# Hash projections of the first batch in float32 from the raw loads, one operation for both lower halves, leaner constants and a new list of places

## The chip, the core and the metric

The kernel runs on one core of a Trainium2 chip. The metric is the device time of one execution in microseconds (us); the shorter, the better. Beside the runs there is one profiled execution, from which all rows below are taken. The engines are TensorE (PE, with its weight loads as PEld), VectorE (DVE), ScalarE (ACT), GpSimd (POOL) and SyncE (SP), which issues most DMAs.

## What is computed

Bucketed attention (4 batches, 8 heads, 768 positions, head width 64), and behind it a feed-forward layer on the 3072 tokens. Cut from the reference:

```python
q_bits = (np.einsum('bhsd,dk->bhsk', q, proj) > 0)      # proj is 64 x 6
k_bits = (np.einsum('bhsd,dk->bhsk', k, proj) > 0)
q_bucket, k_bucket = sum(bits * 2**arange(6))
mask = q_bucket[..., :, None] == k_bucket[..., None, :]
scores = where(mask, 1/8 * q @ k.T, -1e9)
attn = softmax(scores); out = attn @ v                  # then, on (3072 x 512):
h = x @ w_in; g = gelu(h); y = g @ w_out                # w_in 512 x 2048
```

## The kernel before

**Precision.** Everything is float32 at the boundary. A matmul operand is either kept as float32, or held as two parts, an upper and a lower half: for q and k in the type fp32r (tiles `Aq`, `Ak` for the upper, `Bq`, `Bk` for the lower halves), for v, the attention weights and the feed-forward in f16.

**Steps and the list of places.** The program doesn't emit its instructions where it describes them. It describes 3,604 steps (`add`), each with the steps it needs, the engines that could do it, and the ring of buffers it takes a slot of. `Plan.order` then reads the string `ORDER`: three characters for each step, in the order in which the steps were added. The first two are its place (base 64), the third its engine and slot (`ENGINES[way // 8]`, `way % 8`). The steps are emitted in the order of their places, so each engine and each DMA queue gets its instructions in that order and works them off in that order.

**Stages.** The first batch (8 heads) runs through `head_early`, the other three through `head`. Beside the first batch the weights are decoded, scaled and split (`weight_pair`), almost wholly on DVE. Then the feed-forward of a batch is laid between the attention steps of the following batches, and the last batch's feed-forward ends the program.

**One head of the first batch** (`head_early`, L656 on). `raw` is loaded (L664): 128 rows, q above and k below, 768 columns, in one of two single buffers (`raw` for odd heads, `rawe` for even ones). `hi` writes the upper halves of q (times -1/8) and k to `aq`. Three moves (`m1`, `m2`, `m3`) copy halves of `aq` to where the matmuls want them; `lq` and `lk` (L685, L394) write the two lower halves, 64 rows each. The projection (L722 to L724) is three fp32r matmuls that add up in one bank, in two pieces of 256 and 512 columns, with `first_lo`, `first_hi` as weights; a sign on ACT (L727) follows each piece, with the bias `off`; two mask steps `r1`, `r2` write the bits under q and k. The scores (L846) of the head need `m3`, `r1` and `r2`, the projection needs `m1`, `m2`, `lq` and `lk`. `raw` is free when `lq` and `lk` have read it.

**One unit of 128 queries** (`unit`): scores on PE (L846), the least on DVE (L849), exp on ACT (L854); in the first batch then six transposes on PE (L904) with copies out by ACT or DVE (L925), and the product with v in float32 (L984).

**Constants** (L302 to L331): `proj` is sent to 2 x 64 rows by one DMA from ACT's queue (`praw`), `offset` to 2 x 32 rows of one 4-byte word by a second one (`off`). POOL makes `first_hi` and `first_lo` from `praw` with four operations. Two steps (`hash_parts`, `flip_parts`, L419 to L442) make constants for the heads of the later batches from `praw` and `off`.

Of the kernel before, what the change touches and what calls it, by code (L numbers as in the profile page):

```python
# [18 lines left out]
P = 128  # L19
# [4 lines left out]
RAWE = 1  # L24
WHOLE = ((0, 1, 2, 3), (), (), ())
# [9 lines left out]
    "HyYASIAFgAZBAdgAvAAzgBNABSgBuAB2IB7QCABCFICSICYIClIBVgADgAIIAJQALQANQAKIAMIAPoAUBAXQAQAAVQAYQAaIAeAAnIAtQAxoBEABGQA+DBMQ"  # L35
    "AkBArIAwRA2AA4QA9ABAQAyAA5IBDRBHpBLCBZQBTDBcIA3BBBIBJQBjDBnQBQABWQBIABPIBeRBiqBsCBvQBtDByQBUBBgIBpQB1CB+QB4DCCQAEgAOIAbI"
    "AhQAcQATIAWIAmoAqCA7QAsDA1QBOQBCYBlABqIB0RB9rCHDCbQCLACUIBxBB6ICGQCaAChQCWCCeICgQCjICzIC1BC5QAAoCnACsACwADFIDoQDwYCBACKI"
    "CTRC3oDBBDJQDCCDLQCPBCmICtQC6DDDQC4CC8QC2QC7IDZQDfADmRABpDSCDYADcADuIEAQEMYCcACqIDAQDErDMDDdQDQBDbQDIADPIDWQDnBDrQDhDDkQ"
    "DsQD0ID9ID-DECQACqDxBD1AEQAEYIEgYEiYE5hARgAlQApYAoQBRYAuIBFIBYoBbABhQBfCBmQCNQBrYC-BDjIDzQD5pEBAENQEGDEJQDiADpID7REaCEnQ"
    "EWAEbQD8BELIETQEZoEkBEsQEoAEqQEKAEUIEhRExBFAQEtCFBQEeBEmIEuQEzqE6AFEQFCDFHQEpAEvIE4RFGCF3QFFBFSQAggA6YBdYCMYCEgBKIB3YCVo"  # L40
    "CXBCdQCiDCoQDOYCxQE8AFDIFKQFNrFjDFmQFTAFaQE1BE+IFMRFbBFhQFgAFkQFdIFpIFyIF9CF-RFqDFtAFxAGRIGnQHEYFOAFXIFoQF1pGMCGbIF2BF8Q"
    "FWBFeIFsRGECGGQGUDGgQFwIF5IGIYGLAGPIGrBGzAG5AG-IHhIHrYF6AGJIGQQGXrGcAGiQGfBGlQGFBGTIGaRGmDGuIGoCHHQG2QG7IHAYHcDHfRHNCHoA"
    "HuAH2IICIIGYFigBagCRYCkQCvgDTgCZICfYDUoDtAD4QDqDDvQERYEEQGhBGwIG3RG+oHGBHMQHQAHVQGYAGeIGyQHFAHKQHCDHRQG9AHDIHOQHSpHXBHbQ"
    "HnAHwIHIBHPIHWRHmBHqQHiDH0QHdBHpIHvQH1qH6BIHQH9DIAQHUAHjIHsRH4AH8QIDDISQCJgDeQD6gEVYFUgEFIDlYEfoEyDE7QFLDFVQF0QFvQHxAH5I"
    "IBQIIrIOAIUIIMBIfQH+BIEIILRIWCIbQIYDIeIIRQIdIIoIIvCI7QIwBI2AI5AJBIKQQKnYIKAIPIIVQI-oJCDJHQJGBJLIIQBIXIIhRJNDJSQJQBJgQItY"
    "I1II4QI9CJDRJrAJwAJzAJ7IKcQKiYIcAIsIJKQJTrJeAJhQJYDJdQImBI3IJXRJoDJ1QJkBJqQJ6IKSIKUQKqBKvRKIAKLAKhAK1IMLQMMIKohCrgEwYE3g"
    "E9gFZgFQIE-YF4oF+BGDQGOBGWQHBQGpQJUAJnIJuQJ5pKFCKXQJ-BKNQJfBJtIJyRJ+CKAQKBAKEQKCAKGIKKQKOoKpCKsQKRDKWQJ4BKDIKHRKeDKjQKYB"
    "KgQKVAKdIKmRKtqK3BK7QK6DK9QKPBKlIKxQLDALWQLACLEQEOgGNYG0gGxgHkQGkIGVYHLoHYAHgQIFCINQITYIZYKyAK4IK-RLFrLLBLPQLGDLMQK8BLCI"
    "LKQLNCLSQLRDLUQLVQLjILmQLtDLyQLYBLfALlAL0IMGIMJYLHALZILhQLqpLsALuQLvCLzQLTBLeILoRL2DL8QL6CL-IL1QL4IMAQMIDMNQMKBMQAMaAMfI"
    "MtQNPILpALwIL3QL9rMFCMTQL+BMDQLxBL5IMERMdDMhQMRDMXQMYQMiIMsQM+CNLRNIDNOANSANaIP8QSMIAHhAGgAfIAjIA0IBoAAiiA8gBXIBkIBwIB8A"  # L50
    "CDICIICOBCQICpICyIC9IDNQDaIDGYDVIA-hB5iCuIC0IC+IEDCDHhB-gDgID2ID+IEIAESIEXQEdDEjIE0IFIIFPIFYYFrIFfYGAIEHgDXiErIE2IFJIFnA"
    "EPhFRiFuIFzIF7IGCAGHIGKYGSAGZIGdIGjIGsIGvYG1IG6QHZIGBhFcgG8IHJIHTIIaAG4iHegH-IIJIIiIIrAIyII8QJICJOIJbIJiIJmIJpYKrIJvYJ9I"
    "HahIpgJEIJRIJcIKuDJPiJlgKJIKMIKTIKwAK0IK2QK5ALBILIILOILXILcQLkILbYLrIJ2hKfiK+ILJILQIL7AKkgLaiMCIMPIMWIMlAMnIMrQMuCMxIM0I"
    "M6IM8INCQNfINMQNTILghMciMzIM2INBINnDMegNGhNWINdINkINwAN0IN2QN5DN7IOBIOGIOHIOJYOuIORIOoIOkgNJiO8IPBIPEIPwAO5hPKgPYIPcIPnI"
# [136 lines left out]
def tile_bucket_attention_moe(  # L191
# [465 lines left out]
    def head_early(b, h, i, key, clear, cl):  # L657
# [78 lines left out]
        def mask_q():  # L736
            affine(r1.engine, aq[D : D + 2 * NBIT], buf(space)[: 2 * NBIT], 0.5, 0.5)
# [629 lines left out]
```

## Time and profile before

| | us |
|---|---|
| median of 3 runs | 855.67 |
| lowest and highest | 855.56, 857.36 |
| the profiled execution: its own time | 856.2 |
| its span in the trace | 854.4 |

Over the span PE is busy 833.5 us (98%), DVE 681.1 (80%), ACT 641.4 (75%), POOL 69.4 (8%). A busy share of PE is not PE at its peak: the ends of matmuls are modelled, and starts tell the pace better. Times in the rows are us from the start of the span unless they are marked ns.

### The profile page before, as it was taken

To read this page: it belongs to the slowest core of one execution; us is meant where nothing else is said; L and a number is where in the kernel's file an instruction comes from. 1 tells how busy PE (TensorE), PEld (TensorE's weight loads), DVE (VectorE), ACT (ScalarE), POOL (GpSimd) and SP (SyncE) were. 2 spreads that over 40 slices of the span, in tenths; PEclk is the share of its full clock that TensorE was granted. 3 is DMA by queue.
4 is the path that set the end of the run, shared out by engine and by line. 5 is a ranking of instruction groups with operands and counts; after the bars stand their busy time and mean duration, and the time that the engine had idled before them with its cause. 6 is when DMAs were issued, how large, how long until landed. Compare 5 with 4: busy or idle time off the path is not lost.

```text
span 854.4 us, 16603 instructions
## 1 busy us (share of the span) xinstructions
PE 833.5 (98%) x6428; PEld 609.5 (71%) x6428; DVE 681.1 (80%) x1392; ACT 641.4 (75%) x1091; POOL 69.4 (8%) x81
## 2 busy tenths in 40 slices
PE   5899999999999999999999999999999999999998
PEld 3676777857777776777676777677777777676664
DVE  7999999998999999998999989899898771212112
ACT  6898998889898998888988868988878754323232
POOL 3453320102000000000000000000000000000000
PEclk9999999999999999999999999999999999999999
DMA  6775465691996898697979696668869454001000
GB/s 207 224 200 147 148 188 165 130 188 38 187 166 139 164 193 215 118 194 134 185 160 194 165 169 129 150 134 156 182 126 178 94 108 78 1 1 50 2 25 25
DMA packets 270018, 116.56 MB, mean 136 GB/s; under 512 B 228596, under 2 KB 253172, under 8 KB 269940
## 3 DMA queue, kind: packets, MB, share of 16 engines
q1 hardware_dynamic: 269744, 115.50, 61.7%
q8 instruction: 50, 0.82, 0.4%
q14 instruction: 28, 0.23, 0.1%
q10 hardware_dynamic: 196, 0.00, 0.0%
HBM read 41.95 MB, written 6.29 MB: 56 GB/s over the span
## 4 chain that ended last, share of the span: by engine, by line
PE 86%; DVE 6%; DMA 4%; ACT 2%; issue 1%; ACTq 0%; SPq 0%; DVEq 0%
PE hp L1275 28%; PE hp L1196 27%; PE s L846 14%; PE hp L993 8%; PE hp L984 3%; PE hp L904 3%; DVE s L849 2%; PE hp L798 1%; PE hp L799 1%; DMA off<-offset 1%; ACT p L854 1%; DMA wbits<-w_out 1%; DMA vraw<-v 1%; PE hp L505 1%; DMA pt<-hl 1%
## 5 line engine op out<-in xcount | busy, mean ns | idle before, releaser
L1275 PE MATMUL hp<-Wout,g 128*128 128x512 f16 x1152 | 278.5, 380 | 0.0
L1196 PE MATMUL hp<-x,Win 128*128 128x256 f16 x2304 | 272.5, 273 | 0.0
L1196 PEld LDWEIGHTS <-Win 128*128 128x128 f16 x2304 | 219.9, 98 | 46.6 <-issue 11.2
L849 DVE TENSOR_SCALAR_CACHE_REDUCE s<-s 128x768 f32<-128x768 f32 x192 | 182.9, 958 | 14.1 <-PE s L846 12.0
L1275 PEld LDWEIGHTS <-g 128*128 128x128 f16 x1152 | 103.2, 98 | 115.5 <-issue 18.8
L854 ACT ACTIVATE p<-s,rows 128x768 f32<-128x768 f32 x144 | 129.5, 900 | 27.5 <-DVE s L849 10.0
L846 PE MATMUL s<-Ak,Aq 128*128 128x384 f32 x360 | 145.2, 403 | 4.8 <-ACT p L854 3.5
L1206 ACT ACTIVATE h<-hp,ffs 128x512 f32<-128x512 f32 x96 | 65.1, 683 | 98.7 <-PE hp L1196 96.7
L846 PE MATMUL s<-Bk,Bq 128*128 128x384 f32 x360 | 122.0, 339 | 0.0
L1253 DVE SCALAR_TENSOR_TENSOR g<-h,ffs,g 128x512 f16<-128x512 f32 x96 | 70.5, 744 | 28.2 <-ACT g L370 27.1
L846 PEld LDWEIGHTS s<-Ak,Aq 128*128 128x128 f32 x360 | 68.6, 190 | 22.7 <-ACT p L854 7.7
L373 DVE TENSOR_SCALAR g<-h,ffs 128x512 f16<-128x512 f32 x39 | 18.5, 481 | 82.8 <-ACT h L1231 76.5
L993 PE MATMUL hp<-pt,vhl 128*64 128x256 f16 x1296 | 76.1, 274 | 0.0
L993 PEld LDWEIGHTS <-vhl 128*64 128x64 f16 x1296 | 68.7, 110 | 8.4 <-issue 7.8
L846 PEld LDWEIGHTS s<-Bk,Bq 128*128 128x128 f32 x360 | 68.8, 191 | 1.8
L854 ACT ACTIVATE wbits<-s,rows 128x768 f32<-128x768 f32 x48 | 43.1, 898 | 14.1 <-DVE s L849 5.4
L869 DVE SCALAR_TENSOR_TENSOR wbits<-p,rows,wbits 128x768 f16<-128x768 f32 x47 | 47.4, 1011 | 3.6 <-ACT wbits L370 3.3
L869 DVE SCALAR_TENSOR_TENSOR hl<-p,rows,hl 128x768 f16<-128x768 f32 x49 | 49.4, 1009 | 0.3
L1231 ACT ACTIVATE h<-h 128x2048 f32<-128x2048 f32 (+1 forms) x25 | 46.1, 1843 | 0.4
L904 PE MATMUL hp<-ident,p 128*128 128x128 f32 x288 | 43.0, 277 | 0.4 <-ACT pt L370 0.3
L370 ACT ACTIVATE pt<-hp 128x384 f32<-128x384 f32 x86 | 39.1, 490 | 4.5 <-PE hp L904 4.0
L370 ACT ACTIVATE g<-h,ffs 128x512 f16<-128x512 f32 x56 | 39.1, 713 | 1.2 <-PE hp L1275 1.0
(196 smaller groups left out, 1041.4 us busy)
## 6 DMA issues: line engine op xcount, KB each, us to landing
raw<-qk SPq DMA_DIRECT2D x28, 384.0 KB, 4.0
vraw<-v SPq DMA_DIRECT2D x28, 384.0 KB, 4.0
wbits<-w_in SPq DMA_DIRECT2D x16, 512.0 KB, 4.7
wbits<-w_out SPq DMA_DIRECT2D x16, 512.0 KB, 5.0
out<-o SPq DMA_DIRECT2D x11, 512.0 KB, 3.6
Ak<-Aq SPq DMA_DIRECT2D x16, 192.0 KB, 3.3
Bq<-Aq SPq DMA_DIRECT2D x13, 192.0 KB, 3.6
Bk<-Aq SPq DMA_DIRECT2D x12, 192.0 KB, 4.2
```

The lines of the kernel that those rows point to most:

```text
L370: nc.scalar.activation(out=out, in_=in_, func=func, scale=scale, bias=bias)
L846: nc.tensor.matmul(to, x, y, start=k == 0, stop=k == 1)
L849: nc.vector.tensor_scalar(out=both(sp), in0=both(sp), scalar1=BIG / 2, scalar2=None, op0=ALU.min, op1=ALU.min, accum_out=nb,)
L854: nc.scalar.activation(out=buf(ex).rearrange("p (b k) -> p b k", b=2), in_=both(sp), func=AF.Exp, scale=-1.0, bias=nb, accum_out=sums[:, t ...
L869: nc.vector.scalar_tensor_tensor(out=buf(hi)[:, 1], in0=buf(ex), scalar=r, in1=buf(hi)[:, 0], op0=ALU.mult, op1=ALU.subtract,)
L904: nc.tensor.transpose(buf(step[0])[:, (k - k0) * P : (k - k0 + 1) * P], buf(ex)[:, words(k)], ident32,)
L993: nc.tensor.matmul(pv[j * D : (j + 1) * D], buf(vh)[:, tv, kt, j * D : (j + 1) * D], buf(holds[j][0])[:, tp * KT + kt, :nt], start=kt == 0 ...
L1196: nc.tensor.matmul(buf(pair[0])[:, j * ch[1] : (j + 1) * ch[1]], win_hl[:, f0 // WB1, tw, pr, f0 % WB1 : f0 % WB1 + P], x[:, tx, pr, : ch[1]],
L1206: nc.scalar.activation(out=bufs["h"][0][:, 2 * fp : 2 * fp + 2, :nt], in_=buf(pair[0])[:, : 2 * nt].rearrange("p (j k) -> p j k", j=2), fu ...
L1231: nc.scalar.activation(out=h, in_=h, func=AF.Gelu)
L1253: nc.vector.scalar_tensor_tensor(out=gt[:, 1, s2, :nt], in0=h[:, s2, :nt], scalar=sg, in1=gt[:, 0, s2, :nt], op0=ALU.mult, op1=ALU.subtract,)
L1275: nc.tensor.matmul(buf(banks[u]), gt[:, tg, f, u * P : (u + 1) * P], wout_hl[:, ft // UT, tw, ft % UT], start=fresh and f == ti == 0, stop ...
```

## The change

In the first batch all 8 heads (`EXACT = 8`, `JOINT = range(8)`) project `raw` itself with float32 weights `plain`, in one matmul for each piece, and need `raw` alone for it. Both lower halves are written by one DVE operation on 128 rows (`joint_low`) into `bq`; the lower half of k is moved from there to `bk` (`m1`, after `joint_low`), and then the upper half of q goes into the place that it left (`m4`, after `m1`). A head has 14 steps before and after, the scores now need `m1`, `m4` and `joint_low` too, and `raw` is free only when `joint_low` and both pieces of the projection have read it. `proj` is loaded to 64 rows, `offset` by two DMAs of 12 rows each behind a POOL memset; ACT writes `plain` with four operations on 64 x 6, and POOL copies it to `praw`. `flip_parts` and `hash_parts` now need the first batch's signs and projections.

```diff
+EXACT = 8
+JOINT = range(8)
 ORDER = (
...
-    nc.scalar.dma_start(out=praw[:, :NBIT], in_=proj.unsqueeze(0).to_broadcast([2, D, NBIT]))
+    nc.scalar.dma_start(out=praw[:D, :NBIT], in_=proj)
-    nc.scalar.dma_start(out=off, in_=offset.rearrange("(n p) o -> n p o", n=2)[:, :KR])
+    nc.gpsimd.memset(off, 0.0)
+    for n in range(2):
+        nc.scalar.dma_start(out=off[n * KR : n * KR + 2 * NBIT], in_=offset[n * D : n * D + 2 * NBIT])
...
-    first_hi = const.tile([P, KR + HR], F32R, tag="first_hi", name="first_hi")
-    first_lo = const.tile([P, HR], F32R, tag="first_lo", name="first_lo")
+    plain = const.tile([P, HR], F32, tag="plain", name="plain")
+    nc.vector.memset(plain, 0.0)
...
-    nc.gpsimd.tensor_scalar(
-        out=praw[:, NBIT:], in0=praw[:, :NBIT], scalar1=-1.0, scalar2=None, op0=ALU.mult
-    )
-    nc.gpsimd.tensor_copy(out=first_hi[:, KR : KR + 2 * NBIT], in_=praw)
     for rr, cc in sides:
-        nc.gpsimd.tensor_tensor(
-            out=first_lo[rr, cc], in0=praw[rr], in1=first_hi[rr, KR : KR + 2 * NBIT].bitcast(F32), op=ALU.subtract
-        )
+        for n, by in enumerate((1.0, -1.0)):
+            to = slice(cc.start + n * NBIT, cc.start + (n + 1) * NBIT)
+            nc.scalar.activation(out=plain[rr, to], in_=praw[:D, :NBIT], func=AF.Copy, scale=by)
+    for rr, cc in sides:
+        nc.gpsimd.tensor_copy(out=praw[rr], in_=plain[rr, cc])
...
+        def joint_low():
+            nc.vector.scalar_tensor_tensor(
+                out=bq, in0=buf(raw), scalar=fold, in1=aq.bitcast(F32), op0=ALU.mult, op1=ALU.subtract
+            )
...
-        m1 = add_move(S, bq[:D], aq[:D])
-        m2 = add_move(S, bk[D:], aq[D:])
-        m3 = add_move(S, ak[:D], aq[D:])
-        lq = add_low(bq[D:], top, -SCALE)
-        lk = add_low(bk[:D], end)
-        free(raw, [lq, lk])
+        if joint:
+            lows = [add("DVE", subtract_cost("DVE", S), joint_low, key, [hi], port=True)]
+            m2 = add_move(S, bk[:D], aq[D:])
+            m3 = add_move(S, ak[:D], aq[D:])
+            m1 = add_move(S, bk[D:], bq[D:], lows)
+            m4 = add_move(S, bq[D:], aq[:D], [m1])
...
-                nc.tensor.matmul(pp, first_lo, aq[:, n], start=True, stop=False)
-                nc.tensor.matmul(pp, first_hi[:, KR:], bq[:, n], start=False, stop=False)
-                nc.tensor.matmul(pp, first_hi[:, :HR], bk[:, n], start=False, stop=True)
+                nc.tensor.matmul(pp, plain, buf(raw)[:, n], start=True, stop=True)
...
+        if exact:
+            hashed.needs += products
+            flipped.needs += signs
...
+        free(raw, [*lows, *(products if exact else ())])
...
-        return [m3, r1, r2]
+        return [m3, r1, r2, *([m4] if joint else ()), *((m1, *lows) if exact else ())]
```

**What the two lists say**, read with the code of `Plan.order`. For the first head: before, DVE `hi`, `lq`, `lk`, then the second head's `hi`, `flip_parts`, its `lq`, `lk`, then `r2` and a move, then the first weight decode; after, DVE `hi`, `joint_low`, `m1`, the second head's `hi`, `m4`, `r2`, its `joint_low`, then the first weight decode. On ACT before: `m1`, `m2`, `m3`, signs, `r1`; after: the four constants, `m2`, `m3`, signs, `r1`.

Steps placed before the first evacuation of the feed-forward (place 832 before, 826 after), where the counts differ by engine:

| step | DVE before, after | ACT | POOL | SP |
|---|---|---|---|---|
| `hi` of the first batch | 2, 3 | 2, 1 | 4, 4 | |
| lower halves (`lq`, `lk`; `joint_low`) | 11, 8 | | 5, 0 | |
| moves and masks of the first batch | 2, 4 | 17, 18 | 11, 12 | 10, 14 |
| copies of transposes (L925) | 10, 7 | 86, 89 | | |
| `spread` of the divisors | 4, 2 | 6, 9 | 2, 1 | |
| upper halves of x from `rb` | 3, 1 | 7, 9 | 1, 1 | |
| moves and masks of the second batch's heads | | 2, 5 | 2, 1 | 8, 6 |
| upper halves of weights (`high_low`) | | 3, 4 | 7, 6 | |

In the whole program the numbers of steps are the same on PE. The last weight load is step 970 of the list before, its decode 984; after, the last loads are 904 and 966, the decode 992.

## Rows read from the trace of the kernel before

**Rows 1.** Windows by stage: stretch, its length, busy time and instructions of each engine.

```profile
0.00:15.00 15.00, 5.05 (x19) 3.79 (x20) 9.94 (x18) 9.23 (x12) 4.99 (x19) 1.00 0.64 215
15.00:147.50 132.50, 126.96 (x945) 97.91 (x944) 130.61 (x262) 116.66 (x256) 48.40 (x48) 1.00 0.60 176
180.00:200.00 20.00, 18.59 (x121) 11.62 (x120) 16.99 (x36) 16.50 (x24) 1.51 (x2) 1.00 0.68 174
200.00:700.00 500.00, 499.88 (x4018) 369.47 (x4016) 458.20 (x963) 423.08 (x697) 11.05 (x11) 1.00 0.77 155
700.00:854.00 154.00, 150.51 (x1059) 100.11 (x1057) 33.87 (x55) 47.94 (x59) 0.00 (x0) 1.00 0.11 28
```

**Rows 2.** Timeline of the first 14 us: start, length, engine, operation [idle before].

```profile
0.73 1.13 ACTq L302 DMA_DIRECT2D praw<-proj  x1
...
1.89 0.53 ACTq L304 DMA_DIRECT2D off<-offset  x1
...
3.74 0.20 ACT L316 ACTIVATE warm<-ones 128x1 f32<-128x1 bf16 x1
4.11 0.62 DVE L373 TENSOR_SCALAR Aq<-rawe,fold 128x768 fp32r<-128x768 f32 x1 [1.39 <-DMA rawe<-qk]
...
5.70 0.24 POOL L326 TENSOR_SCALAR praw<-praw 128x6 f32<-128x6 f32 x1 [2.07 <-DMA praw<-proj]
...
6.74 0.62 DVE L373 TENSOR_SCALAR Aq<-raw,fold 128x768 fp32r<-128x768 f32 x1
...
7.74 0.65 PE L722 MATMUL hp<-Aq,first_lo 128*44 128x512 f32 x1 [7.74 <-POOL first_lo L331]
...
8.19 0.63 PE L723 MATMUL hp<-Bq,first_hi 128*44 128x512 f32 x1
...
9.57 0.15 DVE L439 TENSOR_SCALAR flips<-off 64x1 f32<-64x1 f32 x1 [2.21 <-DMA off<-offset]
9.66 1.23 ACT L727 ACTIVATE sign<-hp,off,turned 44x512 f32<-44x512 f32 x2 [2.32 <-DMA off<-offset]
...
12.89 0.66 PE L846 MATMUL s<-Ak,Aq 128*128 128x384 f32 x1 [1.16 <-DVE Ak L373]
...
13.25 0.68 DVE L484 TENSOR_SCALAR Win<-wbits 128x1024 int32<-128x1024 int32 x1
```

**Rows 3.** Timeline of PE: the third head's projection, then a product with v.

```profile
25.31 0.32 PE L722 MATMUL hp<-x,first_lo 128*44 128x256 f32 x1
...
26.44 0.27 PE L904 MATMUL hp<-ident,p 128*128 128x128 f32 x1
...
39.05 2.81 PE L984 MATMUL hp<-pt,vhl 128*64 128x256 f32 x24
```

**Rows 4.** Groups by form, 0 to 147.5 us: busy us, mean ns | idle before.

```profile
L373 DVE TENSOR_SCALAR pt<-hp 128x384 f32<-128x384 f32 x10 | 5.5, 546 | 0.1
...
L685 DVE SCALAR_TENSOR_TENSOR Bq<-raw,Aq 64x768 fp32r<-64x768 f32 x4 | 4.7, 1174 | 0.1
...
L776 DVE SCALAR_TENSOR_TENSOR Bq<-raw,fold,Aq 128x768 fp32r<-128x768 f32 x2 | 2.0, 1010 | 0.0
...
L685 DVE SCALAR_TENSOR_TENSOR Bq<-rawe,Aq 64x768 fp32r<-64x768 f32 x2 | 1.9, 952 | 0.1
...
L373 DVE TENSOR_SCALAR Bq<-Aq 64x768 fp32r<-64x768 f32 x1 | 0.6, 552 | 0.0
...
L370 ACT ACTIVATE pt<-hp 128x384 f32<-128x384 f32 x86 | 39.1, 490 | 4.5 <-PE hp L904 4.0
...
L370 ACT ACTIVATE Ak<-Aq 64x768 fp32r<-64x768 f32 x3 | 2.5, 842 | 0.1
...
L394 POOL TENSOR_TENSOR Bk<-raw,Aq 64x768 fp32r<-64x768 f32 x3 | 5.5, 1825 | 3.6 <-ACT Aq L370 3.5
```

**Rows 5.** Timeline of DVE around 181 us.

```profile
181.45 0.76 DVE L484 TENSOR_SCALAR Wout<-wbits 128x512 int32<-128x512 int32 x2 [1.02 <-DMA wbits<-w_out]
```

**Rows 6.** DMA issues: KB each, median us to landing.

```profile
raw<-qk SPq DMA_DIRECT2D x28, 384.0 KB, 4.0
```

More of the change, by code (lines that the diff above doesn't have):

```diff
@@ L39 @@
[L39 to L42, printed above, removed]
@@ L673, in move, with add_move @@
                 affine(on, dst, src.bitcast(F32))
-        def add_move(n, dst, src):
+        def joint_low():
+            nc.vector.scalar_tensor_tensor(
+                out=bq, in0=buf(raw), scalar=fold, in1=aq.bitcast(F32), op0=ALU.mult, op1=ALU.subtract
+            )
+        def add_move(n, dst, src, needs=None):
             box = []
@@ L678, in add_move @@
             box.append(
-                add(on, 0, lambda: move(box[0].engine, dst, src), key, [hi], port=True)
+                add(on, 0, lambda: move(box[0].engine, dst, src), key, needs or [hi], port=True)
             )
@@ L706, in head_early @@
         hi = add(affine_on(f"RND{first}", S, True), 0, high, key, [raw, *clear], port=True)
-        m1 = add_move(S, bq[:D], aq[:D])
-        m2 = add_move(S, bk[D:], aq[D:])
-        m3 = add_move(S, ak[:D], aq[D:])
-        lq = add_low(bq[D:], top, -SCALE)
-        lk = add_low(bk[:D], end)
-        free(raw, [lq, lk])
-        space = add("none", 0, lambda: None, key, [m1, m2, lq, lk], takes="sign")
-        signs = []
+        exact = h < EXACT
+        joint = h in JOINT
+        if joint:
[4 more added lines that the diff above has]
+            m4 = add_move(S, bq[D:], aq[:D], [m1])
+        else:
+            m1 = m4 = add_move(S, bq[:D], aq[:D])
+            m2 = add_move(S, bk[D:], aq[D:])
+            m3 = add_move(S, ak[:D], aq[D:])
+            lows = [add_low(bq[D:], top, -SCALE), add_low(bk[:D], end)]
+        space = add("none", 0, lambda: None, key, [raw] if exact else [m1, m2, *lows], takes="sign")
+        products, signs = [], []
         for c0, c1 in ((0, TC), (TC, S)):
@@ L741, in mask_k @@
             affine(r2.engine, ak[D : D + 2 * NBIT], rows, -BIG / 2, BIG / 2)
-        r1 = add(affine_on(f"MSK{first}", S), 0, mask_q, key, [*signs, m2, m3], port=True)
-        r2 = add(affine_on(f"MSK{first}", S), 0, mask_k, key, signs, port=True)
+        r1 = add(affine_on(f"MSK{first}", S), 0, mask_q, key, [*signs, m2, m3, lows[-1]], port=True)
+        r2 = add(affine_on(f"MSK{first}", S), 0, mask_k, key, [*signs, hi], port=True)
         free(space, [r1, r2])
-        return [m3, r1, r2]
+        return [m3, r1, r2, *([m4] if joint else ()), *((m1, *lows) if exact else ())]
     def head(b, h, i, key, clear, cl):
```

190 lines of the change are left out of this document (99 added, 91 removed).

## Prediction, made before the changed kernel was run

> **What bounds the kernel now.** I read the windows by stage first, because a busy share over the whole span mixes three regimes [rows 1]. In the first 15 us no engine is full: PE works 5.05 us of 15, DVE 9.94. From 15 to 147.5 us DVE is busy 130.61 of 132.5 us (98.6%), PE 126.96 (96%), ACT 116.66 (88%). From 200 us on PE has no gap left (499.88 of 500), and in the last 154 us DVE does only 33.87. So two stages can give time: the start, where everybody waits, and the first batch, where DVE is full. What lies behind the first feed-forward matmul is PE's, and its list of work is not changed. A microsecond by which that point comes sooner is a microsecond at the end, if PE stays full behind it.
>
> Next comes the timeline of the start [rows 2], read backward from the first scores at 12.89. They wait for the masks, those for the signs at 9.66, and the signs for the transfer of `off`: ACT sits idle for 2.32 us and DVE for 2.21, both until `off` has landed. The projection had been released at 7.74 by POOL, which had waited 2.07 us for `praw` and then worked on it from 5.70. Two tiny loads thus set the start, not the 384 KB of q and k: DVE has those at 4.11.
>
> **The start, step by step.** `proj` now goes to 64 rows and is not broadcast twice; its issue takes 1.13 us now. At the worst it lands as before, at 5.70. At the best it takes as long as the first head's load, which DVE had at 4.11. I take 5.2. Then ACT makes `plain` with four tiny operations; the nearest row is 0.20 us each, 0.8 in all, so the weights are there at 6.0 (4.9 to 6.5), where the projection now starts at 7.74. ACT is blocked until then, and `m2` and `m3` are queued behind it: they end near 7.7 (0.84 each [rows 4]), before they are needed.
>
> The float32 matmul's price: 24 records of a product with v take 2.81 us [rows 3]; they are 12 matmuls of 256 columns, two at a time on separate halves of the array. Taken side by side, 256 columns cost 0.47 and a head's 768 columns 1.40; taken one after the other, 0.70. The three fp32r passes cost 1.13 (25.31 to 26.44). So a head's projection changes by -0.4 to +0.27 us; I take +0.27, since the halves write different rows. The Trainium skill, FP8 and Floating Point Precision, TensorE Precision Notes, says that a true float32 product is four passes through the array; by it alone four passes stand against three, 1.5 us for a head instead of 1.13, an estimate from that page, and eight heads would cost PE 0.9 us more than by the rows' 1.40.
>
> All this holds at the pace of 25 us, 0.25 us for 512 columns (1.13 over 2,304). In the first head the starts 7.74 and 8.19 lie 0.45 us apart for 512 columns [rows 2]: that is the lower of TensorE's two levels, 1.2 instead of 2.4 GHz, behind an idle engine, though the granted clock is given as 1.00 for the whole window [rows 1]. So the first head's projection takes some 2.8 us, from 6.0 to 8.8, and its larger piece, which comes first in the list, ends at 7.9.
>
> Signs follow at 7.9 and 8.8 and end near 9.4, if `off` is there. Now 64 single words take from 1.89 to 9.57. Afterwards two transfers of 12 words each do it. Bounds: as late as now, 9.57, or about as fast as `praw`, 5.7. I take the fast end, since few words are left. The Trainium skill, DMA: Bandwidth & Descriptors, Rules for kernel authors, says that the outermost dimension sets over how many DMA engines a transfer is spread, and that a leading broadcast of c copies confines it to c; both loads have an outermost dimension of 2 now. The 7.66 us for 64 words agree with it, and by it `off` would no longer be waited for.
>
> With the mask on ACT (0.84) scores start near 10.3 instead of 12.89. On DVE, which matters more, the first weight decode starts at 13.25 now. The operations ahead of it were `hi`, four lower halves, the second `hi`, the flips, a mask and a move: 0.62 + 4 x 0.95 + 0.62 + 0.63 + 0.55 + 0.55 = 6.8. They become `hi`, two joint ones, `hi`, `m1`, `m4` and the mask: 2 x 0.62 + 2 x 1.01 + 3 x 0.55 = 4.9. `r2` waits for the signs at 9.4, with DVE free at 4.11 + 0.62 + 1.01 + 0.55 + 0.62 + 0.55 = 7.5: an idle time of 1.9 in place of 2.2. The second head's `joint_low` and the decode are queued behind that wait. So the decode starts near 13.25 - 1.9 - 0.3 = 11.0. **Start: -2.2 us** (-1.0 if `off` lands late, -3.2 if `proj` is fast). The flips' 0.63 in it are only put off, and come back below.
>
> **DVE in the rest of the first batch.** Lower halves: 11 operations at 0.95 to 1.17 become 8 at 1.01 [rows 4]; at 0.96, 10.6 become 8.1. One `hi` more, +0.6. Two moves or masks more, +1.1. Three copies of transposes fewer, -1.6. Four fewer operations of 256 columns (two spreads, two upper halves of x), about half a copy each, -1.1, and one more of them for x's lower half, +0.4. In all -3.1, of which 1.3 (6.8 - 4.9, without the flips) are in the start already. **Rest: -1.8 us, and +0.6 for the flips: -1.2.** Bounds: four lower halves on DVE ran at 1.17 rather than 0.95; if that slowing goes with POOL's five lower halves (1.83 each, all removed), 0.9 more is gained; if the joint operations are slowed alike, 1.2 is lost.
>
> **Edits at nothing.** Moves by DMA rise from 10 to 14; a load of twice the size lands in 4.0 us [rows 6], and in the new list the scores stand 40 places or more behind the late moves, which at 832 places in 147 us are 7 us. If that cover went, up to 4 us each would be late in front of a head's first scores. `raw` is held until PE has done both pieces, so the next load, and all loads behind it on SP's queue, wait for PE's order; the pieces stand well ahead of those loads in the list. PE's +0.27 for each head is hidden as long as DVE is the fuller engine; uncovered it is 2.2, or 2.7 with the slow first heads.
>
> **Sum.** -2.2 - 1.2 = **-3.4 us**. The sum is made in the profiled execution (856.2, span 854.4, 1.8 outside the span); it is 0.5 above the median, and the difference carries over: 856.2 - 3.4 = 852.8 for such an execution, 855.67 - 3.4 = **852.3** for the median. Its own range, from the bounds of start and rest, is 850.3 to 854.7.
>
> **Rivals.** *More is won.* DVE waits 1.02 us at 181.45 for the last weights [rows 5], 14 places behind their load; PE has 1.4 us of gaps in that window [rows 1]. The new list has 26 places there. With that, 0.9 from POOL and 1.0 from a fast `proj`: -6.7, **849.0**. Against it: other loads may have become the tight ones. Chance 0.15.
>
> *PE eats it.* PE is at 96% in the stage that DVE is said to bound. If PE sets the pace, the start's 2.2 are left against 2.2 to 2.7 of added matmul time: **855.7**. For it: the shares. Against it: modelled ends make PE look fuller than it is, and DVE's groups show next to no idle time [rows 4]. Chance 0.19.
>
> *ACT becomes the bound (the other side).* ACT gets four moves and masks (3.4 us), three copies (1.5), five smaller ones (at most a copy each, 2), some for the second batch's heads and a weight half, and loses a `hi`: some 7 us on 116.7. My forecast then needs ACT at 94% (123.7 of 131.3). Its copies and exps stand between two of DVE's steps of the same unit, so its waits are not all slack. At 90% the stage takes 137.4: +4.9 - 2.2 = +2.7, **858.4**. It decides from below about 91%. For it: no window in the rows has ACT above 88%. Against it: it had no need to be. Chance 0.14.
>
> The forecast has 0.52. Chances from these: what a measurement of this kernel can tell from no change is about 0.2%, 1.7 us. Faster holds the first two cases, 0.67; same 0.19; slower 0.14. The range runs to 849.0 below and 857.0 above; outside are half of the larger gain and most of the ACT case, under 2 in 10.
>
> **What would show it.** Right: PE's first matmul near 6, no wait for `off`, first scores near 10.3, the first decode near 11, the first feed-forward matmul 3 us sooner, and PE without gaps behind it. Each float32 projection shows 1.4 us of starts for 768 columns. Wrong: DVE still waits past 9.5 (`off`), DVE's idle time before the least-operations grows with ACT as releaser (the ACT case), or DVE's total falls while the first feed-forward matmul stays at its place (PE). A wait for a load or a moved half in front of a head's first scores would be a cost that I set to nothing.

## The result and the profile after

The changed kernel takes 846.74 us (median of 4, 846.35 to 847.10) against 856.51 us for the kernel before, run beside it: a ratio of 0.9888, 95% interval 0.9876 to 0.9901, or 9.6 us less (8.5 to 10.6). The forecast was 3.4 us less. Its sign was right, its size was not: even the rival in which more is won ended at 849.0. The profiled execution has a span of 844.8 us, where 854.4 was the span before.

The windows by stage of the changed kernel, with the columns of [rows 1]:

```profile
core 0: us, PE busy (x) PEld busy (x) DVE busy (x) ACT busy (x) POOL busy (x), PEclk, DMA share, GB/s
0.00:15.00 15.00, 8.22 (x32) 3.78 (x32) 11.77 (x19) 11.55 (x20) 5.23 (x18) 1.00 0.74 239
15.00:147.50 132.50, 130.03 (x983) 100.91 (x984) 126.88 (x268) 123.57 (x275) 40.29 (x40) 1.00 0.65 186
...
180.00:200.00 20.00, 20.00 (x157) 15.19 (x155) 19.01 (x44) 16.02 (x27) 5.43 (x4) 1.00 0.49 108
200.00:700.00 500.00, 499.11 (x4009) 368.03 (x4009) 451.92 (x945) 416.76 (x687) 24.11 (x22) 1.00 0.82 159
```

Read against [rows 1]: in the window from 15 to 147.5 us ACT has gone from 88% to 93% (123.57 of 132.5), DVE from 98.6% to 95.8%, PE to 98%. In the window from 180 to 200 us PE has no gap left, where it had 1.4 us. Behind 200 us little is different.

The first feed-forward matmul, before and after:

```profile
147.35 0.38 PE L1196 MATMUL hp<-x,Win 128*128 128x256 f16 x2
...
131.64 0.60 PE L1218 MATMUL hp<-x,Win 128*128 128x256 f16 x4
```

It starts 15.7 us sooner, where 3 was forecast as a sign. That is the list and not the pace: the new list has 192 score matmuls ahead of it, the old one 204, so its place says nothing of the gain. The window above thus reaches 16 us into the feed-forward in the changed kernel; from 15 to 131.6 us the shares come out the same (ACT 93%, DVE 96%, PE 98%).

The timeline of the start, as in [rows 2]:

```profile
0.74 0.55 ACTq L304 DMA_DIRECT2D praw<-proj  x1
...
1.33 1.19 ACTq L308 DMA_DIRECT2D off<-offset  x2
...
3.99 0.62 DVE L373 TENSOR_SCALAR Aq<-rawe,fold 128x768 fp32r<-128x768 f32 x1 [1.35 <-DMA rawe<-qk]
4.14 0.62 ACT L331 ACTIVATE plain<-praw 64x6 f32<-64x6 f32 x4
...
4.81 2.79 PE L734 MATMUL hp<-rawe,plain 128*44 128x512 f32 x4 [4.81 <-ACT plain L331]
...
6.78 0.68 ACT L737 ACTIVATE sign<-hp,off 44x512 f32<-44x512 f32 x1 [0.43 <-PE hp L734]
...
8.14 0.55 DVE L373 TENSOR_SCALAR Ak<-sign 12x768 fp32r<-12x768 f32 x1 [0.53 <-ACT sign L737]
...
9.03 0.44 PE L868 MATMUL s<-Ak,Aq 128*128 128x384 f32 x1 [1.43 <-ACT Aq L370]
...
9.49 0.34 PE L868 MATMUL s<-Ak,Aq 128*128 128x384 f32 x1
...
9.65 0.69 DVE L484 TENSOR_SCALAR Win<-wbits 128x1024 int32<-128x1024 int32 x1
```

Nobody waits for `off`, and DVE's wait in front of the mask is 0.53 us where I had 1.9. The first scores start 3.9 us sooner than before (9.03 for 12.89), the first decode 3.6 us sooner (9.65 for 13.25).

To see where the rest lies I count score matmuls: each kernel has 768, 24 for each head, and the 97th is the first of the fifth head, near 80 us, half-way through the first batch. The starts, read from the traces (us):

| kernel | first scores | 97th score matmul | between | from there to the end of the span |
|---|---|---|---|---|
| before | 12.89 | 80.3 | 67.4 | 774.1 |
| changed | 9.03 | 71.9 | 62.9 | 772.9 |
| difference | -3.9 | -8.4 | -4.5 | -1.2 |

So by this mark 3.9 us come from the start, 4.5 from the stretch behind it, and 1.2 from the rest. The forecast had 2.2, 1.2 and nothing. The mark is rough, since the two lists lay the scores differently among the other work: the lead is 5.7 us at the 73rd score matmul, 8.4 at the 97th and 5.8 at the 193rd. PE's idle time needs no mark: against [rows 1] it is 3.2 us shorter ahead of 15 us, 3.1 from 15 to 147.5 and 1.4 from 180 to 200, and 0.8 longer behind; PE's busy time is 2.6 shorter (830.9 for 833.5).

In the stretch up to the 97th DVE's groups by form differ most in operations that the change does not touch. Kernel before, 0 to 80.3 us:

```profile
L494 DVE SCALAR_TENSOR_TENSOR Win<-wbits,Win 128x512 int32<-128x512 int32 x2 | 3.6, 1820 | 0.0
L489 DVE SCALAR_TENSOR_TENSOR Wout<-wbits,Wout 128x512 int32<-128x512 int32 x2 | 2.9, 1493 | 0.0
...
L494 DVE SCALAR_TENSOR_TENSOR Wout<-wbits,Wout 128x512 int32<-128x512 int32 x2 | 1.3, 680 | 0.0
```

The changed kernel, 0 to 71.9 us, the same amount of scores:

```profile
L489 DVE SCALAR_TENSOR_TENSOR Wout<-wbits,Wout 128x512 int32<-128x512 int32 x4 | 2.6, 684 | 0.0
L494 DVE SCALAR_TENSOR_TENSOR Wout<-wbits,Wout 128x512 int32<-128x512 int32 x4 | 2.5, 678 | 0.0
```

The same decode step of a weight takes 0.68 us or, in some places before, over twice that. The timeline of the kernel before at such a place:

```profile
28.99 1.82 POOL L394 TENSOR_TENSOR Bk<-raw,Aq 64x768 fp32r<-64x768 f32 x1
...
29.03 2.33 DVE L494 SCALAR_TENSOR_TENSOR Win<-wbits,Win 128x512 int32<-128x512 int32 x1
...
30.89 1.16 POOL L373 TENSOR_SCALAR Bk<-Aq 64x768 fp32r<-64x768 f32 x1
31.28 1.31 DVE L494 SCALAR_TENSOR_TENSOR Win<-wbits,Win 128x512 int32<-128x512 int32 x1
```

The first decode takes 2.33 us instead of 0.68 behind POOL's lower half of k, which ends at 30.81. The second takes 1.31, and it stands behind another POOL operation, a move with one input. The theory I went into the experiments with (contention) saw only the former: the five subtractions on POOL held up DVE's operations, which is more than the lower halves alone. Its rivals: the earlier start is carried to the end; DVE's smaller count; the new places alone.

### The profile page after: what moved, and what is told of

Its sections match the earlier page's. It is cut to its first block, busy times and chain, and to the rows that moved or that the text cites. A ratio compares the mean times of both kernels' runs of the same rounds, so it can differ in the third digit from the quotient of the medians.

```text
span 844.8 us, 16558 instructions
## 1 busy us (share of the span) xinstructions
PE 830.9 (98%) x6412; PEld 605.1 (72%) x6412; DVE 671.9 (80%) x1384; ACT 639.5 (76%) x1098; POOL 78.7 (9%) x86
## 4 chain that ended last, share of the span: by engine, by line
PE 92%; DVE 4%; ACT 2%; DMA 1%; issue 1%; DVEq 0%; ACTq 0%
PE hp L1218 29%; PE hp L1297 29%; PE s L868 15%; PE hp L1015 9%; PE hp L1006 3%; PE hp L926 3%; PE hp L734 1%; DVE s L871 1%; ACT p L876 1%; PE hp L820 1%; PE hp L821 1%; DMA wbits<-w_out 1%; PE hp L505 1%; ACT pt L370 0%; DMA praw<-proj 0%
## 5 line engine op out<-in xcount | busy, mean ns | idle before, releaser
L876 ACT ACTIVATE p<-s,rows 128x768 f32<-128x768 f32 x147 | 132.3, 900 | 25.0 <-DVE s L871 15.9
L373 DVE TENSOR_SCALAR g<-h,ffs 128x512 f16<-128x512 f32 x47 | 21.8, 481 | 102.7 <-ACT h L1253 82.5
L891 DVE SCALAR_TENSOR_TENSOR wbits<-p,rows,wbits 128x768 f16<-128x768 f32 x51 | 51.5, 1011 | 2.1 <-ACT wbits L370 1.7
L876 ACT ACTIVATE wbits<-s,rows 128x768 f32<-128x768 f32 x45 | 40.4, 897 | 13.1 <-DVE s L871 4.3
L926 PEld LDWEIGHTS hp<-ident,p 128*128 128x128 f32 x288 | 33.3, 141 | 6.9 <-issue 1.9
```

The source lines that it names most:

```text
L876: nc.scalar.activation(out=buf(ex).rearrange("p (b k) -> p b k", b=2), in_=both(sp), func=AF.Exp, scale=-1.0, bias=nb, accum_out=sums[:, t ...
L891: nc.vector.scalar_tensor_tensor(out=buf(hi)[:, 1], in0=buf(ex), scalar=r, in1=buf(hi)[:, 0], op0=ALU.mult, op1=ALU.subtract,)
L926: nc.tensor.transpose(buf(step[0])[:, (k - k0) * P : (k - k0 + 1) * P], buf(ex)[:, words(k)], ident32,)
```

## The experiments

Differences in us are ratio minus one, times 856; "before" and "changed" are the two kernels. The changed kernel was not timed again beside these runs, so a distance from it is given twice, by medians and by ratios; each ratio is good to some 1.3 us.

**Loads alone.** Before, with the lean loads.

```diff
-    nc.scalar.dma_start(out=praw[:, :NBIT], in_=proj.unsqueeze(0).to_broadcast([2, D, NBIT]))
+    for n in range(2):
+        nc.scalar.dma_start(out=praw[n * D : (n + 1) * D, :NBIT], in_=proj)
-    nc.scalar.dma_start(out=off, in_=offset.rearrange("(n p) o -> n p o", n=2)[:, :KR])
+    nc.gpsimd.memset(off, 0.0)
+    for n in range(2): ... 12 words of offset each
```

> The kernel before, with nothing but the lean loads: proj by two DMAs of 64 rows, off's two hash vectors by a memset and two DMAs of 12 rows. If the early start is kept to the end (theory: start), the first sign no longer waits for off at 9.66, the first decode of a weight starts 1 to 2 us earlier than 13.25, and the end comes 0.7 to 1.9 us earlier, about 854.9. If the start is swallowed by a later stage that is full anyway (rival), the end stays within 0.5 us of 856.5.

855.30 us, ratio 0.9987 (0.9978 to 0.9996): 1.1 us less. First scores at 11.53, 1.4 sooner, but the 97th only 0.6 sooner (79.7). The start is worth something in the old kernel; at the 97th half of it is lost, though the end by the times has most of it.

**POOL's lower halves on DVE.** Before; only the engine letter of five entries in the list differs.

> The kernel before, with the five lower halves of k that POOL computed (heads 3 to 7) put on VectorE at the same places; the same subtraction. Plain count (rival): VectorE, full in the first batch, gets five operations of about 0.96 us more, so the end is 4.8 us later, about 861. If POOL's two-input subtraction held VectorE up (theory: contention), the decodes and the least sums of the first 81 us fall from a mean of 1.1 to 1.25 us to about 0.68, 4 to 6 us are given back, and the end is between 1.5 us earlier and 1.5 us later.

857.56 us, ratio 1.0016 (1.0006 to 1.0025): 1.4 us more, where five operations of 0.95 us were added to a full engine. Some 3.4 us are given back. The decodes of 128x512 fall to 0.85 us in the mean of eight (1.17 before), and the copy `diag`, which has one input, from 1.38 to 0.29. The decodes of `Win` stay near 1.0 in the mean, so the subtractions were not all that held them.

**One input in place of two on POOL.** Before.

```diff
-  lambda: subtract(box[0].engine, out, buf(raw)[rows], aq[rows].bitcast(F32)),
+  lambda: subtract(...) if box[0].engine == "DVE" else affine("Pool", out, buf(raw)[rows], 2.0**-12),
```

> The kernel before, with the five lower halves of k on POOL (heads 3 to 7) made by one multiplication of the raw rows by a constant in place of the subtraction of two tensors; the lower halves of k in those heads, and so their hashes, are other numbers. If the second input is what holds VectorE up, the slow decodes beside it go back to 0.68 us and the end is 3 to 5 us earlier, about 852.5. If any operation of POOL does it, the decodes stay near 1.2 us and the end within 1 us of 856.5.

852.76 us, ratio 0.9960 (0.9945 to 0.9975): 3.4 us less (2.1 to 4.7). Groups by form of this run, 0 to 77.5 us:

```profile
L494 DVE SCALAR_TENSOR_TENSOR Win<-wbits,Win 128x512 int32<-128x512 int32 x2 | 2.6, 1320 | 0.0
...
L373 POOL TENSOR_SCALAR Bk<-raw 64x768 fp32r<-64x768 f32 x3 | 2.5, 831 | 0.2
```

The gain is as the theory has it, but the decodes are at 1.32 us, not at 0.68, one behind the new POOL operation and one behind the move that follows it, and POOL's operation has become shorter too (0.83 for 1.83). Whether the second input or the time on POOL does it stayed open here; the last experiment takes it up.

**TensorE kept busy.** Before, with 54 matmuls of ones ahead of the list.

```diff
+    for _ in range(54):
+        nc.tensor.matmul(bufs["hp"][3][:, :P], ones, ones, start=True, stop=True)
```

> The kernel before, with 54 matmuls of 128x128 bfloat16 ones into a free PSUM tile ahead of the list, so that TensorE works while it would wait for the first loads. If the lower clock level of the first 18.8 us costs the chain time, the first scores take 0.175 us a matmul instead of 0.32 from the start, and the end is 1 to 3 us earlier, about 854.5. If VectorE's full stage behind it takes that up (rival), the end stays within 0.5 us of 856.5.

857.16 us, ratio 1.0010 (1.0001 to 1.0019): no gain. The first projection of this run, and two windows:

```profile
7.73 0.43 PE L725 MATMUL hp<-Aq,first_lo 128*44 128x512 f32 x1 [1.29 <-POOL first_lo L331]
8.00 0.40 PE L726 MATMUL hp<-Bq,first_hi 128*44 128x512 f32 x1
...
5.70:12.50 6.80, 2.49 (x24) 1.65 (x22) 4.44 (x10) 4.46 (x6) 1.83 (x5) 1.00 0.64 236
12.50:16.00 3.50, 3.18 (x11) 3.05 (x12) 3.43 (x7) 2.67 (x4) 1.34 (x1) 0.51 0.96 297
```

TensorE worked from 0.99 to 6.4 us and did reach the upper level, 2.4 GHz: the starts of the first projection lie 0.27 us apart where they lay 0.45 (7.74 and 8.19). But the signs still wait for `off` (until 9.59), TensorE stands mostly idle from 9.0 to 12.8 us, and from 12.5 to 16 us the granted clock is 0.51, the lower level of 1.2 GHz, so the first scores start 0.32 us apart as before. A faster first projection is worth nothing while `off` is late; what faster first scores would be worth, this run doesn't tell.

**POOL's subtraction put back.** Changed, in heads 3 to 7; what it writes is written over by `m3`.

```diff
         def high():
             affine(hi.engine, aq, buf(raw), fold)
+            if h > 2:
+                subtract("Pool", ak[:D], buf(raw)[D:], aq[D:].bitcast(F32))
```

> The changed kernel, with one POOL subtraction of two tensors (64x512 words, as the old lower half of k had) put back behind the upper half in heads 3 to 7; its result is written over before anything reads it. Contention theory: VectorE's decodes beside it go from 0.68 to over 1 us again, and the end is 3 to 5 us later than the changed kernel's 846.7, about 851. Rival (POOL's operation runs beside the others and costs nothing): within 0.5 us of 846.7.

849.16 us, ratio 0.9911 (0.9896 to 0.9926): 2.4 us above the changed kernel by the medians, 2.0 by the ratios, a little under what was expected (the operation has 64x768 words, not 64x512). The timeline of this run at two of the five places:

```profile
28.10 1.83 POOL L394 TENSOR_TENSOR Ak<-raw,Aq 64x768 fp32r<-64x768 f32 x1 [0.50 <-DVE Aq L373]
28.14 2.61 DVE L678 SCALAR_TENSOR_TENSOR Bq<-rawe,fold,Aq 128x768 fp32r<-128x768 f32 x1
...
30.87 1.00 DVE L678 SCALAR_TENSOR_TENSOR Bq<-raw,fold,Aq 128x768 fp32r<-128x768 f32 x1
...
39.43 1.83 POOL L394 TENSOR_TENSOR Ak<-raw,Aq 64x768 fp32r<-64x768 f32 x1
...
40.02 2.33 DVE L494 SCALAR_TENSOR_TENSOR Wout<-wbits,Wout 128x1024 int32<-128x1024 int32 x1
41.36 1.97 POOL L373 TENSOR_SCALAR Win<-Win,tiny 128x1024 f16<-128x1024 f32 x1
42.27 1.87 DVE L678 SCALAR_TENSOR_TENSOR Bq<-raw,fold,Aq 128x768 fp32r<-128x768 f32 x1
```

POOL's subtraction takes 1.83 us at each of these places, where it is ahead. DVE's joint operation that starts just behind it takes 2.61 instead of 1.00; the decode at 40.02 takes 2.33 instead of 1.22, and POOL's ends at 41.26, 1.24 us into it. DVE does most of its work only when POOL is through: 0.82 of the 1.00 us, 1.08 of the 1.22. The joint operation at 42.27 takes 1.87, and it stands behind an operation of POOL with one input that ends at 43.33.

**The old load of `off` alone.** Changed, `off` again by one DMA of 2 rows of 32 words.

> The changed kernel, with off loaded as before by one DMA of 2 rows broadcast over 32 words. The first sign waits for it again, until about 9.5 instead of 6.78. If a late start lasts to the end, the end is 1.5 to 2.7 us later than 846.7, about 849; if a later stage swallows it, within 0.5 us of 846.7.

846.21 us, ratio 0.9880 (0.9866 to 0.9895): no difference, and not for the reason given. `off` was not late at all. Timeline of this run:

```profile
6.92 0.68 ACT L735 ACTIVATE sign<-hp,off 44x512 f32<-44x512 f32 x1 [0.43 <-PE hp L732]
...
9.65 0.52 PE L866 MATMUL s<-Bk,Bq 128*128 128x384 f32 x1
...
9.97 0.52 PE L866 MATMUL s<-Ak,Aq 128*128 128x384 f32 x1
...
10.29 0.52 PE L866 MATMUL s<-Bk,Bq 128*128 128x384 f32 x1
```

The same transfer that took until 9.57 in [rows 2] has landed by 6.92. What differs is the transfer of `proj` ahead of it on ACT's queue. The run shows another thing by chance: its first scores go at half pace, 0.32 us apart, those of the changed kernel at 0.17 (9.31, 9.49, 9.66), and the ends are the same.

**Projections twice.** Changed, each float32 projection issued twice.

> The changed kernel, with each float32 hash projection of the first batch issued twice, the same result. If TensorE sets the time in the first batch, eight times 1.4 us, about 11 us, is added, 858. If the other engines cover the projections, under 3 us is added.

855.12 us, ratio 0.9983 (0.9974 to 0.9993): 8.4 us above the changed kernel, for 8 times 1.4 us (longer in the first head). First scores start at 11.59, so 2.6 of it lie in the first head. PE was busy 131.43 us of the window from 15 to 147.5, DVE 122.21. Nothing covers this much of TensorE's time.

**New operations at the old places.** Changed, with the old list; a step that would come ahead of what it needs moves back to the first place where it can stand.

```diff
-        steps = sorted(self.steps, key=lambda s: s.start)
+        waiting = sorted(self.steps, key=lambda s: s.start)
...
+            for s in waiting:
+                if all(n.seq in done for n in s.needs) and (not s.takes or (s.takes, s.slot) in free):
+                    break
```

> The changed kernel's operations and loads at the places of the old list: the operation on both lower halves where the one of q stood, the two moves that need it behind it, every other step where it stood before, and steps that would come ahead of what they need put right behind it (some 18 steps move back, loads above all). If the operations carry the gain (no POOL subtraction, 8 lower halves for 11, early start), the end is near the changed kernel, 846 to 849. If the new list carries part of it, the end is between, 850 to 853; if nearly all, above 854.

869.44 us, ratio 1.0158 (1.0139 to 1.0177): 13.5 us slower than before, outside everything that was expected. The chief waits of this run, 0 to 160 us (us in total, times, longest):

```profile
POOL Aq L385 <- DMA raw<-qk: 22.3, 2, 12.6
...
DVE Wout L496 <- DMA wbits<-w_out: 7.4, 2, 4.7
...
ACT Aq L382 <- DMA Ak<-Aq: 4.5, 1, 4.5
```

The operations that fit the new list stall on the old one, on transfers: a raw head is now held until its projection is done, so its buffer comes free later in the list, and the raw loads of the first batch stand up to 64 places further back; what SP has to issue behind them goes back too. Up to the 73rd score matmul this run is ahead of the kernel before (60.2 for 62.1 us); then come the stalls, 9 us by the 97th. By this run the gain can't be divided into operations and places: on the old list, with its steps put back in this way, the operations bring none of it.

**Both old loads.** Changed, with `proj` and `off` loaded as before.

> The changed kernel with both constants loaded as before: proj by one DMA broadcast over two halves, off by one DMA of 2 rows of 32 words. The copies of proj and the first projection wait for proj, and the signs for off, as before until about 9.6. If the start counts, the first scores come near 12 instead of 9.03 and the end 1 to 3 us later than 846.7, about 848.7. If the VectorE work behind takes it up (in the kernel before, an earlier start of 1.4 us was worth 1.1), under 1 us.

848.54 us, ratio 0.9912 (0.9895 to 0.9929): 1.8 us above the changed kernel by the medians, 2.1 by the ratios. Timeline of this run:

```profile
0.73 1.16 ACTq L304 DMA_DIRECT2D praw<-proj  x1
...
1.92 0.54 ACTq L306 DMA_DIRECT2D off<-offset  x1
5.48 0.62 ACT L329 ACTIVATE plain<-praw 64x6 f32<-64x6 f32 x4 [1.50 <-DMA praw<-proj]
...
9.66 1.04 ACT L735 ACTIVATE sign<-hp,off 44x512 f32<-44x512 f32 x2 [1.97 <-DMA off<-offset]
```

`off` is late again, with `proj` broadcast ahead of it. First scores at 11.63, 2.6 later, and the span of the profiled execution, the slowest of the four, is 2.6 longer (847.4): here most of a late start is lost.

**Lower halves split.** Changed; the joint operation of heads 0 to 2 as two of 64 rows, 11 in place of 8.

```diff
+            for rows in (slice(0, D), slice(D, P)) if h < 3 else (slice(0, P),):
                 nc.vector.scalar_tensor_tensor(
-                    out=bq, in0=buf(raw), scalar=fold, ...
+                    out=bq[rows], in0=buf(raw)[rows], scalar=fold[rows], ...
```

> The changed kernel with the joint lower halves of heads 0 to 2 made by two VectorE operations of 64 rows each, so 11 operations in place of 8, as VectorE had before. If VectorE sets the pace of the first batch, three operations of some 0.95 us more make the end 2.5 to 3 us later, about 849.5. If another engine does, under 1 us.

849.07 us, ratio 0.9920 (0.9905 to 0.9935): 2.3 us above the changed kernel by the medians, 2.7 by the ratios. Six halves at 1.09 us in place of three joint ones at 1.01 are 3.5 us of DVE; some 70% of it is paid.

**All three undone.** The old loads, the split and POOL's subtractions in one kernel.

> The changed kernel with three things undone at once: the old loads, 11 VectorE operations for the lower halves, and the five POOL subtractions. Each undone alone took 1.8 us (loads), 2.3 (three operations) and 2.5 (POOL). If they add up on one engine that is full, VectorE, the end is about 6.6 us later than 846.7, 853.3, and some 3 us of the change lie elsewhere. If they share one cover, each hiding the next, the end is under 851. If they make up the whole change, 856.

852.53 us, ratio 0.9964 (0.9951 to 0.9976): 5.8 us above the changed kernel by the medians, 6.5 by the ratios, and 3.1 below before. They add up, nearly: 1.8 + 2.3 + 2.4 = 6.5 by the medians. First scores at 11.43, the 97th at 78.6: 67.1 us between, 4.2 more than in the changed kernel on the same list.

**A fifth more of each projection.** Changed, with one more float32 matmul over the first fifth of each half's columns.

```diff
+                few = slice(n.start, n.start + (n.stop - n.start) // 5)
+                nc.tensor.matmul(pp[:, : few.stop - few.start], plain, buf(raw)[:, few], start=True, stop=True)
```

> The changed kernel with one more float32 matmul of the first fifth of each half's columns ahead of each projection, written over by it: some 0.27 us more of TensorE a head, 2.2 in all, which is what the float32 projections take beyond the three passes before. If TensorE's time is paid as in the run with whole projections issued twice (8.7 for some 11.2), 1.7 us more than 846.7. If VectorE covers this little, within 0.5 us.

847.75 us, ratio 0.9908 (0.9893 to 0.9923): 1.0 us above the changed kernel by the medians, 1.7 by the ratios. About half of the 2.2 us or more is paid. In the trace 0.6 of it lies ahead of the first scores (9.63 for 9.03), where the first head's addition runs at the lower level. The stretch from there to the 97th is 63.2 us for 62.9; as it is 62.5 and 63.0 in two runs that change only loads, this trace can't tell what the other heads pay.

**The same POOL time with one input.** Changed, with two multiplications by a constant in each of heads 3 to 7, where the run above had one subtraction.

```diff
+            for n in range(2 if h > 2 else 0):
+                affine("Pool", ak[:D], buf(raw)[D:], 2.0**-12)
```

> The changed kernel with two POOL multiplications of 64x768 by a constant (one input, 0.83 us each in an earlier run) put back in each of heads 3 to 7, where another run had one subtraction of two tensors (1.83 us) and ended 2.4 us later; what they write is written over before anything reads it. If only POOL's second input holds VectorE up, the end is within 0.7 us of 846.7. If any POOL operation that already runs holds a VectorE operation with two SBUF inputs until it has ended, the joint operations and decodes beside these are 0.5 to 1.6 us longer too, and the end 1.5 to 2.5 us later, about 848.8.

846.97 us, ratio 0.9893 (0.9876 to 0.9910): no difference that can be told. Timeline of this run, the same place as above:

```profile
38.93 0.83 POOL L373 TENSOR_SCALAR Ak<-raw 64x768 fp32r<-64x768 f32 x1
...
39.52 1.31 DVE L494 SCALAR_TENSOR_TENSOR Wout<-wbits,Wout 128x1024 int32<-128x1024 int32 x1
...
39.84 1.68 POOL L373 TENSOR_SCALAR Ak<-raw 64x768 fp32r<-64x768 f32 x1
...
40.76 1.57 DVE L678 SCALAR_TENSOR_TENSOR Bq<-raw,fold,Aq 128x768 fp32r<-128x768 f32 x1
...
59.23 1.22 DVE L494 SCALAR_TENSOR_TENSOR Wout<-wbits,Wout 128x1024 int32<-128x1024 int32 x1
...
59.42 1.55 POOL L394 TENSOR_TENSOR x<-rb,x 128x256 f16<-128x256 f32 x1
```

The first multiplication is ahead of the decode, ends 0.24 us into it and holds it for 0.1. The second starts behind the decode and takes 1.68 us instead of 0.83: here POOL waits. When the joint operation starts, POOL needs another 0.77 us, and the joint operation is 0.56 longer. At 59.42 even a subtraction of two tensors waits for DVE, 1.55 us instead of 0.67.

So the number of inputs on POOL is not what decides. In this run and in those above, a DVE operation is longer by what is left of the POOL operation ahead of it, less 0.1 to 0.2 us. Behind subtractions it is 1.61 us longer with 1.79 left (28.14), and 1.11 with 1.24 (40.02); behind operations with one input 0.87 with 1.06 (42.27), and 0.56 with 0.77 (40.76). What makes the subtraction dear is that it lasts 1.83 us in one piece; of two short operations the second often comes behind DVE's and waits itself. Taken against the middle duration of each form, DVE's operations that start beside one of POOL's are about 6 us longer in sum up to the 97th score matmul in the kernel before, 4.5 with the subtractions put back, 2.1 here and 1.1 in the changed kernel. At the two thirds that such time costs, the 1.0 us here is 0.7 at the end, which these times can't tell from nothing.

## Why the prediction was wrong in its size, step by step

**What bounds the first batch: right, but not alone.** DVE's time counts: 3.5 us more of it cost 2.3 to 2.7. But TensorE's counts as well, at 98% of the stage. One window for the whole stage hid this. The kernel before in two halves:

```profile
15.00:75.00 60.00, 54.69 (x398) 41.74 (x397) 59.25 (x110) 51.09 (x111) 28.36 (x23) 1.00 0.70 206
75.00:147.35 72.35, 72.12 (x547) 56.04 (x546) 71.26 (x153) 65.42 (x146) 20.05 (x25) 1.00 0.52 150
```

Up to 75 us PE is busy 91% beside a full DVE; from there on it has 0.2 us of gaps.

**The step that failed: "Rest: -1.2", and its bound "0.9 more is gained".** Between the first scores and the 97th the change gave 4.5 us. The part counted from operations was near: 11 lower halves to 8, 2.5 us of DVE in the working, where the split's 3.5 us cost 2.3 to 2.7. What was mis-sized is POOL. I saw that four lower halves ran at 1.17 us, tied this to POOL's subtractions, and bounded it by those four, 0.9 us, outside the forecast. The tie was wrong: two of the four are slow, one behind a move (22.56, 1.47 us), one behind a lower half of x (54.91, 1.32), and none behind a lower half of k. Those held other operations: two decodes, at 2.33 and 2.30 us instead of 0.68, and `diag`, at 1.38 instead of 0.29, 4.4 us in all; the other two of the five held nothing. Measured, POOL's subtractions cost 3.4 us in the old kernel against one-input operations of 0.83 us, and 2.0 to 2.4 put back into the new one. The row was there to be read: decodes of one size with means of 0.68 and 1.82 in the same stage. I looked only at groups that the change touches. The Trainium skill, SBUF — State Buffer, Who interferes with whom, says that a VectorE instruction with two SBUF inputs contends with a GpSimd instruction that reads SBUF, and that the order of issue, not the shape of the operation, decides who waits. The traces agree: 2.61 us beside POOL's unchanged 1.83 where POOL is ahead, POOL's 1.68 for 0.83 where DVE is, and DVE held by one-input operations too (1.87 and 1.57 for 1.01).

**The start: right in mechanism, too small.** "I take 5.2" for `proj` was 4.14 or sooner, since `plain` starts then with no wait; four tiny copies took 0.62, not 0.8; the projection took 2.79 us (2.8 predicted), from 4.81 and not 6.0. Scores came at 9.03, not 10.3. The -2.2 should have been -3.6 to -3.9. Undoing the loads accounts for 2.6 of it (11.63 for 9.03). With the old loads scores still come 1.3 us sooner than before (11.63 for 12.89). That isn't the projection, since the signs start at 9.66 in both; it is DVE's mask, which starts at 10.74 behind the signs, and in the kernel before at 12.19, behind both lower halves of the second head. My reading that few words make `off` fast was wrong in its cause: 64 single words land in time too, when no broadcast `proj` goes ahead of them. Nor is the outermost dimension of 2, with which I explained the 7.66 us, enough by itself, as that run has it too.

**"PE's +0.27 is hidden": wrong in the first head, open behind it.** About as much TensorE time added once more cost 1.0 to 1.7 us of 2.2, 0.6 of it in the first head. The price was near: a later head's projection shows 1.31 us of starts for 768 columns (from 18.73: 0.47 for 256, twice 0.42 for 512), where I had 1.40. What the change itself pays behind the first head no run shows by itself.

**What adds up.** The forecast is short by 6.2 us. The start makes 1.4 to 1.7 of it, POOL 2.0 to 3.4, and PE's gap behind the first batch, below, 1.4. Undone together, loads, lower halves and POOL are 5.8 to 6.5 of the 9.6 us, and 3.1 are left. The 1.5 us by which first scores still come sooner then (11.43) and the gap of 1.4 would fill that; no run undid these two, so this part is argued.

**Behind the first batch: the wait that I left to a rival.** DVE's wait for the last weights [rows 5] is gone, and PE's gap of 1.4 us with it; behind the 97th score matmul 1.2 us are gained. The gap stays in the three runs on the old list that change loads or lower halves (PE 18.58, 18.66 and 18.54 of 20 us in that window; 19.53 with TensorE kept busy) and is gone in all on the new list (19.93 to 20.00) and in the run of the new operations at the old places (20.00, though all of it is shifted by some 15 us there). Two runs on the old list speak against the list alone: with TensorE kept busy, and with the new operations at the old places, DVE doesn't wait for the last weights either. So the cause of this gap stays open. I had this at 1.0 us with a chance of 0.15.

**The rivals.** *More is won* named all three sources, but took each at its smallest and stopped at 849.0. *PE eats it* was half true: PE takes some of its time, but DVE's gain is not stopped. *ACT becomes the bound* is false: ACT runs at 93% of the stage, where I had said that it decides below 91%.

**Edits at nothing.** The moves by DMA and the raw rows held longer cost little on the new list: POOL waits 2.1 us once for a moved half, and DVE 0.9 once for a weight (at 53.57), which it does in no other run on this list. The run on the old list lost all of the gain and 13.5 us more, with waits for raw loads, weights and a moved half. The cover that I named, places far ahead of the need, was the condition.

## What to carry to other kernels

When an engine is full, read its groups by form over the whole stage, not only those that the change touches: one form with two durations may show that another engine is stopping it, and the work to remove may stand on that other engine, idle as it looks. Then look at the single instructions: a mean of two hid that one took 0.68 us and the other 2.30. A long operation on POOL beside a full VectorE costs more than its place on POOL suggests; moving five to VectorE cost 1.4 us for 4.8 us of work. And when operations change in an order written out by hand, the old order says nothing about the new operations: when a buffer is held longer, the loads behind it must be placed anew.

## What the runs showed of the hardware that was not expected

- VectorE and GpSimd hold each other up, and the one that starts second waits. A DVE operation with two SBUF inputs behind a POOL subtraction of two tensors takes 2.61 us instead of 1.00, 2.33 instead of 1.22, 2.33 instead of 0.68; behind a POOL operation with one input 1.87 instead of 1.01, 1.31 instead of 0.68. POOL's multiplication behind a decode takes 1.68 us instead of 0.83, its subtraction 1.55 instead of 0.67. The least-operation on scores (PSUM) keeps its 0.96 us, as at 49 us in the kernel before; the copy `diag`, with one input, doesn't (1.38 for 0.29).
- One transfer of 2 rows of 32 single words was there by 6.92 us behind a lean transfer and at 9.66 behind a broadcast one; the broadcast takes 1.16 us to issue instead of 0.55. That the two share DMA engines is argued, not shown.
- First scores at 0.32 us apart, the lower of TensorE's levels, or at 0.17, with 846.21 and 846.59 us for the two executions: the level of the first few microseconds was not what set the time. Matmuls put ahead from 0.99 us did raise it (starts 0.27 us apart for 0.45), but behind a TensorE that stood mostly idle from 9.0 us on it had fallen again when the first scores came (0.51 granted).
